# First h phase of a fused attention and gated feed-forward kernel rearranged: single PSUM banks, two early output accumulators, and the general loop from batch 2

## The chip, the cores and the metric

The kernel runs on one core of one Trainium2 chip. The metric is the device time of one execution in microseconds (us); the median of several runs is compared. "PE" is the matmul engine (TensorE) and "PEld" its weight load, "DVE" is VectorE, "ACT" is ScalarE, "POOL" is GpSimd, "SP" is SyncE, which only issues DMAs here. PSUM has eight banks; a bank holds 512 fp32 values for each of 128 partitions.

## The reference

There are 8 batches, 8 heads, 576 rows and 64 columns in a head. A small set p of 32 packed rows attends to k and v, and q then attends to the packed rows. The result, laid out as 4608 x 512, goes through a feed-forward of width 2048 with the gate h·cos(h).

```
def sm_attn(qq, kk, vv):
    s = scale * np.matmul(qq, kk.transpose(0, 1, 3, 2))
    a = exp(s - max(s));  a = a / sum(a)
    return np.matmul(a, vv)
p_packed = sm_attn(p, k, v)                  # 8 x 8 x 32 x 64
x = sm_attn(q, p_packed, p_packed)           # as 4608 x 512
h = x @ w_in                                 # 512 x 2048
out = (h * np.cos(h)) @ w_out                # 2048 x 512
```

## The kernel before

**Stages of one batch b.** The kernel never forms x. It makes, in this order:

- kT, qT: k and q with the head dimension on partitions. Two ways: `pe_T` (L94, 24 PE transposes in three groups of eight, each group copied from PSUM by the engine named) or `xbar` (L90, one DMA transpose issued by SP).
- `s1(b)` (L133): scores of p against k, then exp on ACT into a1, with row sums; `recips(b)` (L143): two small DVE instructions.
- a1T: a1 transposed, by PE (`a1_pe` L154, `a1_one` L164) or by a DMA transpose (`a1_xbar` L149).
- `permute_v(b)` (L85): one copy of v into another order, vp, on POOL (on DVE for batch 0).
- `pp(b)` (L172): 24 matmuls of 64 columns from vp and a1T, evacuated to ppT by four small copies.
- `ppw(b, n)` (L189): ppT times columns n*512 to n*512+512 of w_in, 8 matmuls, evacuated to PPW. Four of them for each batch.
- `s2(b)` (L215): scores of q against the packed rows, exp to a2u; `sums2` (L222): column sums by a matmul with ones, then Ln; `normalise(b)` (L232): two exps on ACT and two products on DVE give a2n.
- `h_mm(b, fc)` (L242), for fc = 0 to 15: four matmuls of 288 columns give h for 128 of the 2048 columns and 576 rows in a pair of PSUM banks; ACT makes cos (L254), DVE multiplies (L257) into gT. After fc 7 and fc 15 POOL copies the last 64 rows of two batches side by side into `joint` (L261).
- output chunks (`out_gen`, L295): a chunk is 128 rows, 16 matmuls of 512 columns over fc into one bank, then a copy to osb and the DMAs to the output from SP. A batch has four chunks; an odd one has a fifth, from `joint`, for two batches. One output matmul is one unit of filler: `fill(n)` issues n of them between the other work.

**Order.** The instructions of each engine run in program order; there is no scheduler. PSUM is shared by pool `psA` (three pairs of banks, L50), which serves nearly everything, and pool `psO` (two single banks, L51), for output chunks and, at the start, for `bank()` users (`own=True`).

**Opening** (L343 to L396): loads, batch 0 up to a2n, batch 1 up to a1T. `warm` issues dummy matmuls. All loads go through POOL's DMA queue in program order. The times at which POOL issues them show that it waits for the landing of the eighth load before (the issue of w_out's third quarter, at 19.91 us, is released by w_in's first quarter, for example).

**h phase of batch 0** (L397 to L408): 16 times `h_mm(0, fc)`, with ppw(0, 1..3) behind fc 1, 5, 8, pp(1) behind 10, the transposes of q of batch 1 behind 11 to 13, `set_filler(0)` behind 13, and two filler units behind 14 and 15.

**Front of batch 1** (L431 to L448): s2, ppw, sums2, normalise for batch 1, with 22 units of filler; k of batch 2, q of batch 2 and k of batch 3 go through `xbar`.

**Slot of batch 1** (L449, `slot` L410): 16 times h_mm(1, fc) with filler of batch 0 shared out between them and hooks behind given fc.

**Stage of batch 2** (L452 to L483): written by hand. It makes s1, a1T, pp, s2, ppw of batch 2 and also s1 and a1T of batch 3, with 80 units of filler of batch 1, and then runs the slot of batch 2.

**General loop, from batch 3** (L485 to L516): s2(s), ppw(s, 2), the DMA transpose of q(s+1), 8 units, s1(s+1), ppw(s, 3), the DMA transpose of a1(s+1), the DMA transpose of k(s+2), a one-element copy `gate` on POOL that waits for that k, 9 units around sums2, normalise(s), 13 units, the loads of later batches, and the slot with pp(s+1) behind fc 5 and ppw(s+1, 0..1) behind fc 10. `permute_v(s + 1)` stands at the head of the loop.

Of the kernel before, what the change touches and what calls it, by code (L numbers as in the profile page):

```python
# [15 lines left out]
def kernel(  # L16
# [38 lines left out]

    w_in_bf = const.tile([128, 4, DF], BF16, name="w_in_bf")
# [19 lines left out]
            eng.tensor_copy(out=out, in_=in_)  # L76
# [164 lines left out]

    def h_mm(b, fc):  # L242
        if fc == 0:
            gT[b] = g_pool.tile([128, NFC, S], BF16, name="gT", tag="gT")
# [11 lines left out]
        def rest():  # L256
            V.tensor_tensor(out=gT[b][:, fc, :].rearrange("p (e x) -> p e x", e=2),  # L257
                            in0=ps[:, :, 0:HS], in1=csv, op=ALU.mult)
# [182 lines left out]
    xbar("k", 2)  # L441
    xbar("q", 2)
    xbar("k", 3)
    G.tensor_copy(out=gate, in_=xT["k", 3][0:1, 0, 0:1])
    load("q", 3)
# [3 lines left out]
    slot(1, [(3, lambda: pw2(1, 2, (ACT, V))), (6, lambda: pack_p(2, 5)), (8, lambda: pack_p(5, B)),  # L449
             (8, lambda: (permute_v(2), load("v", 3), load("k", 4)))], 4)  # L450

    fill(1000)  # L452
    set_filler(1)
    ACT.preload_act_table_set(EXP_SET)
    s1(2)
    fill(10)
# [3 lines left out]
    recips(2)  # L460
    fill(3)
    s1(3)
    pp(2)
    a1_xbar(3)
    recips(3)
    fill(6)
    s2(2)
    ppw(2, 0, V)
    xbar("q", 3)
    xbar("k", 4)  # L470
    fill(4)
    sums2(2, 0)
    ppw(2, 1, V)
    sums2(2, 1)
    normalise(2)
    G.tensor_copy(out=gate, in_=a2n[2][0:1, 1, 0:1])
    permute_v(3)
    fill(8)
    G.tensor_copy(out=gate, in_=xT["k", 4][0:1, 0, 0:1])
    for n, b in (("v", 4), ("q", 4), ("k", 5)):  # L480
        load(n, b)
    fill(8)
    slot(2, [(3, lambda: pw2(2, 2, (ACT, V))), (7, lambda: pp(3, engs=(ACT, ACT))), (11, lambda: pw2(3))], 5, {11: 3})  # L483

    for s in range(3, B):  # L485
        nxt = s + 1 < B
        fill(1000)
# [8 lines left out]
        fill(8)
        if nxt:
            s1(s + 1)
            ppw(s, 3, V)
            a1_xbar(s + 1)  # L500
            recips(s + 1)
            if s + 2 < B:
                xbar("k", s + 2)
                G.tensor_copy(out=gate, in_=xT["k", s + 2][0:1, 0, 0:1])
# [45 lines left out]
```

## Time and profile before

| what | value |
|---|---|
| time, median of 3 runs | 254.6 us (254.18, 254.6, 256.1) |
| profiled execution: span from first to last instruction | 252.3 us (its only own time) |
| PE / ACT / DVE / POOL busy, share of the span | 92% / 68% / 65% / 23% |
| granted TensorE clock, mean over the span | 0.997 |
| loads by POOL's queue, each k, q or v (576 KB) | 8 each, median 12.2 / 9.6 / 7.4 us to landing |
| the four quarters of w_in, of w_out (512 KB) | 16.5, 20.9 us to landing (median) |
| DMA transposes of k, q, a1 | 6, 6, 5; median 5.3, 6.6, 4.0 us to landing |

Times of a position are us from the start of the span. A row of the timeline has the start, the length, the engine, the source line, the instruction with its operands, its count, and in brackets how long the engine had been idle before it and what released it. Several instructions in a row are merged; since matmuls are pipelined, the length of the last one overlaps what follows. A row of the table of windows gives, for a stretch of the span, its length and then the busy time and the count of instructions of each engine, the granted TensorE clock as a share, the busy share of the DMA engines, and GB/s.

### The profile page before, as it was taken

How to read it: one execution, taken by the hardware profiler on the slowest of the kernel's cores; microseconds unless marked ns; L12 is line 12 of the kernel's file. 1: busy time of each engine (PE TensorE's matmuls, PEld its weight loads, DVE VectorE, ACT ScalarE, POOL GpSimd, SP SyncE). 2: the span in 40 equal slices, each digit the busy share in tenths (PEclk: the TensorE clock that was granted, in tenths of full speed). 3: DMA queues.
4: the chain of work that ended last, by engine and by line, in shares of the span. 5: the costliest groups of instructions: out<-in, count | busy, mean ns of one | idle time of the engine just before them, and what ended most of it. 6: DMA issues, size and time to landing. Idle time of an engine off the chain costs nothing.

```text
span 252.3 us, 4989 instructions
## 1 busy us (share of the span) xinstructions
PE 233.3 (92%) x1981; PEld 130.7 (52%) x2014; DVE 163.0 (65%) x245; ACT 170.5 (68%) x285; POOL 58.4 (23%) x71
## 2 busy tenths in 40 slices
PE   8786888999969999999999998999899999999993
PEld 3453463566435554465446553565356554665452
DVE  2548996789376977477847675479556874876110
ACT  2366888857558788878886667887877585873000
POOL 8442604200362243104313105020500000000000
PEclk9999999999999999999999999999999999999998
DMA  6999999999999989999999994979471112112133
GB/s 91 202 211 205 205 207 226 200 186 149 191 208 198 176 175 212 220 204 164 225 173 181 180 182 99 175 141 196 97 144 44 42 44 70 36 34 62 50 83 83
DMA packets 65270, 37.67 MB, mean 149 GB/s; under 512 B 37872, under 2 KB 60656, under 8 KB 65248
## 3 DMA queue, kind: packets, MB, share of 16 engines
q0 software_dynamic: 23184, 18.81, 48.8%
q1 hardware_dynamic: 41904, 18.42, 36.8%
q8 instruction: 15, 0.25, 0.4%
q10 hardware_dynamic: 160, 0.13, 0.2%
q14 instruction: 7, 0.06, 0.1%
HBM read 37.22 MB, written 9.44 MB: 185 GB/s over the span
## 4 chain that ended last, share of the span: by engine, by line
PE 74%; DVE 8%; ACT 7%; DMA 5%; issue 2%; POOL 2%; DVEq 0%; POOLq 0%; ACTq 0%
PE ot L303 42%; PE psA L250 22%; DMA w_in_bf<-in_moe_w_in_dram 5%; DVE gT L257 5%; PE psA L201 3%; ACT cosT L254 3%; PE psA L177 2%; PE psA L227 1%; PE ot L289 1%; ACT a2u L219 1%; ACT L489 1%; DVE rs L147 1%; PE psA L128 1%; DVE osb L76 1%; DVE PPW L76 1%
## 5 line engine op out<-in xcount | busy, mean ns | idle before, releaser
L303 PE MATMUL ot<-w_out_bf,gT 128*128 128x512 bf16 x483 | 126.9, 380 | 2.1 <-issue 1.3
L257 DVE TENSOR_TENSOR gT<-psA,cosT 128x576 bf16<-128x576 f32 x128 | 94.1, 754 | 31.1 <-ACT cosT L254 30.0
L254 ACT ACTIVATE cosT<-psA 128x576 bf16<-128x576 f32 x128 | 82.7, 652 | 29.8 <-PE psA L250 28.1
L250 PE MATMUL psA<-a2n,PPW 128*128 128x288 bf16 x512 | 84.0, 286 | 2.5 <-DVE PPW L76 1.0
L303 PEld LDWEIGHTS <-gT 128*128 128x128 bf16 x512 | 48.0, 98 | 42.6 <-issue 6.1
L250 PEld LDWEIGHTS <-PPW 128*128 128x128 bf16 x512 | 49.1, 98 | 36.5 <-issue 3.8
L76 DVE CAST PPW<-psA 128x1024 bf16<-128x1024 f32 (+1 forms) x23 | 25.8, 1128 | 12.1 <-PE psA L201 12.1
L261 POOL COPY joint<-gT 128x512 bf16<-128x512 bf16 x16 | 9.8, 614 | 88.7 <-DVE gT L257 88.7
L76 DVE COPY osb<-ot 128x512 f32<-128x512 f32 (+1 forms) x19 | 12.8, 671 | 16.9 <-PE ot L303 13.8
L74 ACT COPY osb<-ot 128x512 f32<-128x512 f32 (+1 forms) x18 | 10.3, 571 | 18.7 <-PE ot L303 14.1
L76 POOL COPY vp<-vbf 96x3072 bf16<-96x3072 bf16 x7 | 19.2, 2750 | 1.6 <-DMA vbf<-in_v_dram 1.6
L237 DVE SCALAR_TENSOR_TENSOR a2n<-a2u,r,lns 128x576 bf16<-128x576 bf16 x16 | 12.4, 813 | 9.6 <-ACT lns L235 9.6
L229 ACT ACTIVATE lns<-psA 128x576 f32<-128x576 f32 x16 | 10.3, 651 | 5.7 <-PE psA L227 5.3
L137 ACT ACTIVATE a<-psA 128x576 bf16<-128x576 f32 x16 | 10.2, 648 | 5.0 <-PE psA L128 5.0
L303 PE MATMUL ot<-w_out_bf,joint 128*128 128x512 bf16 x46 | 12.4, 380 | 0.1
L201 PE MATMUL psA<-w_in_bf,ppT 64*32 64x512 bf16 x224 | 10.4, 381 | 1.5 <-DVE gT L257 1.1
L219 ACT ACTIVATE a2u<-psA,rs 128x576 bf16<-128x576 f32 x16 | 11.0, 736 | 1.2 <-PE psA L128 1.1
L254 ACT ACT_TABLE_LOAD x8 | 10.3, 1283 | 0.1
L74 ACT CAST ppT<-psA 64x128 bf16<-64x128 f32 x24 | 6.2, 259 | 6.1 <-PE psA L103 2.9
L235 ACT ACTIVATE lns<-lns 128x576 f32<-128x576 f32 x16 | 10.0, 678 | 0.0
L341 PE MATMUL ot<-wz 128*128 128x512 bf16 x24 | 8.1, 472 | 1.5 <-DVE wz L353 1.2
L74 ACT CAST PPW<-psA 128x1024 bf16<-128x1024 f32 (+1 forms) x9 | 7.2, 826 | 2.6 <-PE psA L201 2.6
(71 smaller groups left out, 143.4 us busy)
## 6 DMA issues: line engine op xcount, KB each, us to landing
kbf<-in_k_dram POOLq DMA_DIRECT2D x8, 576.0 KB, 12.2
vbf<-in_v_dram POOLq DMA_DIRECT2D x8, 576.0 KB, 7.4
qbf<-in_q_dram POOLq DMA_DIRECT2D x8, 576.0 KB, 9.6
out_dram<-osb SPq DMA_DIRECT2D x24, 192.0 KB, 2.6
out_dram<-osb SPq DMA_DIRECT2D x22, 128.0 KB, 2.4
w_in_bf<-in_moe_w_in_dram POOLq DMA_DIRECT2D x4, 512.0 KB, 16.5
w_out_bf<-in_moe_w_out_dram POOLq DMA_DIRECT2D x4, 512.0 KB, 20.9
out_dram<-osb SPq DMA_DIRECT2D x26, 64.0 KB, 2.1
```

What stands on the lines that cost most here:

```text
L74: ACT.copy(out=out, in_=in_)
L76: eng.tensor_copy(out=out, in_=in_)
L137: ACT.activation(out=a1[b % 2][:, y, :, 0:TP].rearrange("p (e m) x -> p e m x", e=2), in_=ps[y][:, :, 0:HS].rearrange("p e (m x) -> p e m ...
L201: nc.tensor.matmul(ps[y][32 * x:32 * x + 32, :], ppT[b % 2][r, 2 * x + y, :], w_in_bf[r, x, n * 512:(n + 1) * 512], start=True, stop=True)
L219: ACT.activation(out=a2u[b][:, y].rearrange("p (e x) -> p e x", e=2), in_=ps[y][:, :, 0:HS], func=AF.Exp, scale=rs1[b][:, y:y + 1])
L229: ACT.activation(out=lns[b][:, y].rearrange("p (e x) -> p e x", e=2), in_=ps[:, :, 0:HS], func=AF.Ln)
L235: ACT.activation(out=lns[b][:, y], in_=lns[b][:, y], func=AF.Exp, scale=-1.0)
L237: V.scalar_tensor_tensor(out=a2n[b][:, y], in0=a2u[b][:, y], scalar=r1[b][:, y:y + 1], in1=lns[b][:, y], op0=ALU.mult, op1=ALU.mult)
L250: nc.tensor.matmul(ps[:, e, 0:HS], PPW[b][:, y, fc * 128:(fc + 1) * 128], a2n[b][:, y, e * HS:(e + 1) * HS], start=(y == 0), stop=(y == 1))
L254: ACT.activation(out=csv, in_=ps[:, :, 0:HS], func=AF.Sin, bias=PI_HALF)
L257: V.tensor_tensor(out=gT[b][:, fc, :].rearrange("p (e x) -> p e x", e=2), in0=ps[:, :, 0:HS], in1=csv, op=ALU.mult)
L303: nc.tensor.matmul(pss[c], w, w_out_bf[:, fc, :], start=(fc == 0), stop=(fc == NFC - 1))
```

## The change

**PSUM.** `psA` can be closed and opened again. `banks(3)` gives three pairs as before; `banks(1)`, in force only during the h phase of batch 0, gives one pair and four single banks (`psH`).

**h phase of batch 0.** `h_one` takes the first 512 rows only: two matmuls of 512 columns into one single bank, cos and product on 512. The other 64 rows are made later by one `h_rest(0)`: 32 matmuls of 64 columns into one pair, one cos and one product of 1024, straight into `joint` (so batch 0 needs no POOL copies). pp(1) and the transposes of q of batch 1 leave the phase. `set_filler(0)` moves to behind fc 3, and one filler unit follows each of fc 4 to 11: the two output banks hold chunks 0 and 1 from there on. ppw(0, 2) and ppw(0, 3) use the psA pair.

**Loads.** The first quarter of w_out moves ahead of the third and fourth of w_in; v of batch 1 moves behind w_in; k of batch 2 and the rest of p move ahead of the other three quarters of w_out.

**Opening.** The transposes of q(0) and k(1) go to the two single banks; normalise(0) and s1(1) stand ahead of ppw(0, 0).

**Front of batch 1.** It now also makes pp(1), the PE transposes of q(1) and k(2), s1(2), recips(2), a1T(2) by PE. It has 11 units of filler. Only q(2) and k(3) go through `xbar`.

**Slot of batch 1.** Hooks: ppw(1, 2..3) behind fc 1, h_rest(0) behind 4, pack_p behind 6, pp(2) behind 9, ppw(2, 0..1) behind 12. It has the 45 units left of batch 0.

**General loop from batch 2.** The stage written by hand is gone. In the loop, permute_v(3) does not stand at the head for s = 2 but behind normalise(2); on POOL it thus follows the gate copy that waits for k of batch 4.

```diff
-    A = ctx.enter_context(tc.tile_pool(name="psA", bufs=3, space=PSUM))
+    def banks(pairs):
+        psum["stack"].close()
+        psum["A"] = psum["stack"].enter_context(tc.tile_pool(name="psA", bufs=pairs, space=PSUM))
+        if pairs < 3:
+            psum["H"] = psum["stack"].enter_context(tc.tile_pool(name="psH", bufs=6 - 2 * pairs, space=PSUM))
...
+    def h_one(b, fc):
+        if fc == 0:
+            g_tile(b)
+        ps = psum["H"].tile([128, 512], FP32, name="psH", tag="H")
+        for y in range(2):
+            nc.tensor.matmul(ps, PPW[b][:, y, fc * 128:(fc + 1) * 128], a2n[b][:, y, 0:512],
+                             start=(y == 0), stop=(y == 1))
+        cs = cos_pool.tile([128, 512], BF16, name="cosT")
+        ACT.activation(out=cs, in_=ps, func=AF.Sin, bias=PI_HALF)
+        V.tensor_tensor(out=gT[b][:, fc, 0:512], in0=ps, in1=cs, op=ALU.mult)
+
+    def h_rest(b):
+        t = psa()
+        for fc in range(NFC):
+            for y in range(2):
+                nc.tensor.matmul(t[:, fc // 8, (fc % 8) * 64:(fc % 8) * 64 + 64],
+                                 PPW[b][:, y, fc * 128:(fc + 1) * 128], a2n[b][:, y, 512:576],
+                                 start=(y == 0), stop=(y == 1))
+        cs = cos_pool.tile([128, 2, 512], BF16, name="cosR", bufs=1)
+        ACT.activation(out=cs, in_=t, func=AF.Sin, bias=PI_HALF)
+        j0 = (b % 2) * 64
+        V.tensor_tensor(out=joint[b // 2][:, :, j0:j0 + 64],
+                        in0=t.rearrange("p a (f x) -> p (a f) x", x=64),
+                        in1=cs.rearrange("p a (f x) -> p (a f) x", x=64), op=ALU.mult)
...
-    for n in range(3):
-        load_w_in(n)
+    load_w_in(0)
+    load_w_in(1)
+    load_w_out(0)
...
+    load_w_in(2)
+    load_w_in(3)
     load("v", 1)
-    load_w_in(3)
...
-    pe_T("q", 0, (V, ACT, V))
+    pe_T("q", 0, (V, ACT, V), own=True)
     load("q", 1)
-    for n in range(4):
-        load_w_out(n)
+    load("k", 2)
     G.dma_start(out=p_raw[:, 4:, :], in_=p_rows[:, 4:, :])
+    for n in range(1, 4):
+        load_w_out(n)
...
-    load("k", 2)
     permute_v(1)
+    banks(1)
     for fc in range(NFC):
-        h_mm(0, fc)()
-        if fc in (1, 5, 8):
-            ppw(0, 1 + fc // 4, (ACT, V), own=True)
-        if fc == 10:
-            pp(1, own=True, engs=(ACT, ACT))
-        if fc in (11, 12, 13):
-            pe_T("q", 1, (V, ACT, V), (fc - 11,), own=True)
-        if fc == 13:
+        h_one(0, fc)
+        if fc in (1, 5, 9):
+            ppw(0, 1 + fc // 4, (ACT, V), own=fc == 1)
+        if fc == 3:
             set_filler(0)
-        if fc >= 14:
-            fill(2)
+        if 4 <= fc < 12:
+            fill(1)
+    banks(3)
...
+    pp(1)
     ACT.preload_act_table_set(EXP_SET)
+    pe_T("q", 1, (V, ACT, V))
     s2(1)
+    load("v", 2)
     load("q", 2)
     load("k", 3)
-    load("v", 2)
     dup_p(4, 2 * B, G)
-    fill(8)
+    ppw(1, 0, V)
+    pe_T("k", 2, (V, ACT, V))
     sums2(1, 0)
     sums2(1, 1)
...
+    pack_p(2, 5)
+    fill(2)
+    normalise(1)
+    s1(2)
+    recips(2)
     ppw(1, 1, V)
-    normalise(1)
-    fill(14)
...
+    fill(6)
     a1_pe(2, (0,))
     fill(3)
     a1_pe(2, (1,))
...
+    xbar("q", 2)
+    xbar("k", 3)
+    def behind_k3():
+        permute_v(2)
+        load("v", 3)
+        G.tensor_copy(out=gate, in_=xT["k", 3][0:1, 0, 0:1])
+        load("q", 3)
+        load("k", 4)
+    behind_k3()
+    slot(1, [(1, lambda: pw2(1, 2, (ACT, V))), (4, lambda: h_rest(0)), (6, lambda: pack_p(5, B)),
+             (9, lambda: pp(2, engs=(ACT, ACT))), (12, lambda: pw2(2))], 4, {12: 2})
-    for s in range(3, B):
+    for s in range(2, B):
...
-        if nxt:
+        if nxt and s > 2:
             permute_v(s + 1)
...
         normalise(s)
+        if s == 2:
+            permute_v(3)
         fill(13)
```

More of the change, by code (lines that the diff above doesn't have):

```diff
@@ L49 @@
     small = ctx.enter_context(tc.tile_pool(name="small", bufs=3))
-    A = ctx.enter_context(tc.tile_pool(name="psA", bufs=3, space=PSUM))
     O = ctx.enter_context(tc.tile_pool(name="psO", bufs=2, space=PSUM))
     ctx.enter_context(tc.manual_schedule())
+    psum = {"stack": ctx.enter_context(ExitStack())}
+    def banks(pairs):
[4 more added lines that the diff above has]
+    banks(3)
     V, ACT, G = nc.vector, nc.scalar, nc.gpsimd
@@ L78, in psa @@
     def psa(dt=FP32):
-        return A.tile([128, 2, 512 if dt == FP32 else 1024], dt, name="psA", tag="A")
+        return psum["A"].tile([128, 2, 512 if dt == FP32 else 1024], dt, name="psA", tag="A")
     def load(n, b):
@@ L243, in h_mm @@
         if fc == 0:
-            gT[b] = g_pool.tile([128, NFC, S], BF16, name="gT", tag="gT")
-            if b % 2 == 0:
-                joint[b // 2] = j_pool.tile([128, NFC, 128], BF16, name="joint", tag="joint")
+            g_tile(b)
         ps = psa()
@@ L263, in h_mm, with g_tile @@
         return rest
+    def g_tile(b):
+        gT[b] = g_pool.tile([128, NFC, S], BF16, name="gT", tag="gT")
+        if b % 2 == 0:
+            joint[b // 2] = j_pool.tile([128, NFC, 128], BF16, name="joint", tag="joint")
+    def h_one(b, fc):
+        if fc == 0:
+            g_tile(b)
+        ps = psum["H"].tile([128, 512], FP32, name="psH", tag="H")
[18 more added lines that the diff above has]
+                        in1=cs.rearrange("p a (f x) -> p (a f) x", x=64), op=ALU.mult)
     n_out = [0]
@@ L374 @@
     pp(0)
-    pe_T("q", 0, (V, ACT, V))
+    pe_T("q", 0, (V, ACT, V), own=True)
     load("q", 1)
-    for n in range(4):
+    load("k", 2)
+    G.dma_start(out=p_raw[:, 4:, :], in_=p_rows[:, 4:, :])
+    for n in range(1, 4):
         load_w_out(n)
-    G.dma_start(out=p_raw[:, 4:, :], in_=p_rows[:, 4:, :])
     s2(0)
@@ L384 @@
     sums2(0, 1)
-    pe_T("k", 1, (V, V, V))
+    pe_T("k", 1, (V, V, V), own=True)
     pack_p(1, 2, bank(BF16))
     warm(2)
+    normalise(0)
+    s1(1)
     cut_ppw, rest_ppw = ppw(0, 0, V, own=True, later=True, cuts=((0, 128), (128, 512)))
-    normalise(0)
     cut_ppw()
-    s1(1)
     a1_one(1)
@@ L394 @@
     recips(1)
-    load("k", 2)
     permute_v(1)
+    banks(1)
     for fc in range(NFC):
-        h_mm(0, fc)()
-        if fc in (1, 5, 8):
-            ppw(0, 1 + fc // 4, (ACT, V), own=True)
-        if fc == 10:
-            pp(1, own=True, engs=(ACT, ACT))
-        if fc in (11, 12, 13):
-            pe_T("q", 1, (V, ACT, V), (fc - 11,), own=True)
-        if fc == 13:
+        h_one(0, fc)
+        if fc in (1, 5, 9):
+            ppw(0, 1 + fc // 4, (ACT, V), own=fc == 1)
+        if fc == 3:
             set_filler(0)
-        if fc >= 14:
-            fill(2)
+        if 4 <= fc < 12:
+            fill(1)
+    banks(3)
     def slot(s, hooks, keep=0, heavy={}):
@@ L429, in tk @@
         return lambda: pe_T(n, b, (V, V, V), (i,))
+    pp(1)
     ACT.preload_act_table_set(EXP_SET)
+    pe_T("q", 1, (V, ACT, V))
     s2(1)
-    ppw(1, 0, V)
+    load("v", 2)
     load("q", 2)
     load("k", 3)
-    load("v", 2)
     dup_p(4, 2 * B, G)
-    fill(8)
+    ppw(1, 0, V)
+    pe_T("k", 2, (V, ACT, V))
     sums2(1, 0)
     sums2(1, 1)
[L441 to L445, printed above, removed]
-    ppw(1, 1, V)
-    normalise(1)
-    fill(14)
[L449 to L456, printed above, removed]
+    pack_p(2, 5)
[3 more added lines that the diff above has]
+    recips(2)
+    ppw(1, 1, V)
+    fill(6)
     a1_pe(2, (0,))
@@ L459 @@
     a1_pe(2, (1,))
[L460 to L483, printed above, removed]
-    for s in range(3, B):
+    xbar("q", 2)
[10 more added lines that the diff above has]
+    for s in range(2, B):
         nxt = s + 1 < B
```

## The prediction

> **What bounds the kernel now.** I read the page's busy shares first, then the chain that ended last, then a table of windows cut at the stage borders, then the timelines of PE, SP, POOL and DVE around them.
>
> ```profile
> PE 233.3 (92%) x1981; PEld 130.7 (52%) x2014; DVE 163.0 (65%) x245; ACT 170.5 (68%) x285; POOL 58.4 (23%) x71
> ...
> PE 74%; DVE 8%; ACT 7%; DMA 5%; issue 2%; POOL 2%; DVEq 0%; POOLq 0%; ACTq 0%
> ```
>
> PE is 92% busy and 74% of the chain: time is lost only where PE stands still. The windows say where (busy times there are lengths of pipelined matmuls, so they hide short gaps).
>
> ```profile
> 22.70:40.10 17.40, 14.30 (x168) 8.48 (x167) 15.50 (x26) 14.40 (x26) 6.03 (x6) 1.00 1.27 206
> 40.10:45.70 5.60, 5.44 (x33) 2.51 (x35) 3.95 (x4) 4.88 (x8) 2.44 (x4) 1.00 1.25 221
> 45.70:63.90 18.20, 17.71 (x133) 10.77 (x133) 15.04 (x22) 11.89 (x20) 1.60 (x2) 1.00 1.32 179
> 63.90:79.40 15.50, 12.91 (x144) 6.25 (x147) 9.21 (x14) 10.38 (x20) 6.57 (x8) 1.00 1.09 200
> 79.40:98.40 19.00, 18.39 (x162) 10.80 (x164) 14.60 (x20) 14.98 (x26) 5.84 (x6) 1.00 1.13 185
> ...
> 123.90:152.30 28.40, 28.08 (x233) 15.53 (x236) 19.02 (x27) 20.30 (x35) 6.50 (x8) 1.00 1.02 176
> ```
>
> Rows: h phase 0; front 1; slot 1; front and slot of the hand-written stage 2; stage 4 of the general loop. PE is open in the first (DVE 15.5 of 17.4 us) and the fourth; stage 4 is nearly closed.
>
> ```profile
> 24.60 0.75 DVE L257 TENSOR_TENSOR gT<-psA,cosT 128x576 bf16<-128x576 f32 x1
> ...
> 38.86 0.76 DVE L257 TENSOR_TENSOR gT<-psA,cosT 128x576 bf16<-128x576 f32 x1 [0.17 <-ACT cosT L254]
> ```
>
> h phase 0 runs on DVE from 24.6 to 39.6: 0.94 us for each of 16 column blocks.
>
> ```profile
> 71.44 0.76 PEld L177 LDWEIGHTS <-vp 96*128 96x128 bf16 x24 [2.52 <-POOL vp L76]
> ```
>
> The largest single PE wait of stage 2: pp(2) waits for permute_v(2) on POOL. Now the general loop, stage 4, which begins with s2 at 123.86:
>
> ```profile
> 123.86 0.44 PE L128 MATMUL psA<-qT,ppT 64*32 64x288 bf16 x16
> ...
> 137.53 0.86 PE L177 MATMUL psA<-a1T,vp 96*128 96x64 bf16 x24
> ```
>
> ```profile
> 125.58 3.48 SPq L92 DMA_TRANSPOSE qT<-qbf  x1
> 129.15 1.98 SPq L151 DMA_TRANSPOSE a1T<-a  x1
> 131.24 3.05 SPq L92 DMA_TRANSPOSE kT<-kbf  x1
> ```
>
> ```profile
> 124.51 2.75 POOL L76 COPY vp<-vbf 96x3072 bf16<-96x3072 bf16 x1
> 136.30 0.18 POOL L504 COPY gate<-kT 1x1 bf16<-1x1 bf16 x1 [9.03 <-DMA kT<-kbf]
> ```
>
> pp comes 13.7 us after the stage's s2, the POOL gate 12.4 after it; the vp copy is long done, because it stands ahead of the gate.
>
> **The change, part by part.** Pitches on PE, from merged rows: filler 0.216 us (13 in 2.97, less a lone 0.38, over 12); h_mm 0.49, ppw 0.34, pp 0.70 (pieces of the chain); a matmul of 64 columns 0.029 (0.70 over 24); 24 transposes 1.03 (from 1.19); s1 or s2 0.26 to 0.35; a1T by PE 0.35 for each half; sums2 0.25; six pack transposes 0.34. DVE: 576-wide products follow each other every 0.67 us (two in 1.41, less 0.76), 512-wide PPW copies every 0.60 (29.73 to 30.33); a 512-wide product I take as 0.60. ACT: cos 0.55 pitch, at 512 wide about 0.49.
>
> *A, opening to 24.6: 0.* Load order: POOL's issues at 19.91, 22.41, 24.97 and 27.91 mark landings of w_in's first three quarters and v(1), 2.5 us for a quarter, 2.9 for a k, q or v. In the new order: w_in 1 and 2 at 19.8 and 22.3 as before, w_out's first quarter 24.9, w_in 3 and 4 at 27.5 and 30.0, v(1) 32.9 (before 27.9), q(1) 35.8, k(2) 38.7, rest of p 40.8, the w_out quarters 43.4, 46.0, 48.6, then v(2) 51.4, q(2) 54.3, k(3) 57.2. The new order of normalise(0), s1(1), ppw(0, 0), and k(1) through two single banks, shift things by 0.2 us at most either way.
>
> *B, h phase 0: −3.1 us.* DVE has 16 × 0.60 + 3 × 0.60 = 11.4 us in place of 16 × 0.67 + 3 × 0.60 + two q copies of 0.5. Four single banks: one tile's round is about 0.6 (two matmuls with their latency) + 0.6 cos + 0.7 product + 0.4 hand-overs = 2.3, over four 0.58: just under 0.60, so DVE sets the pace. I add 0.5 for ppw(0, 2), whose w_in lands at 27.5 when DVE is in column block 4. End 24.6 + 11.4 + 0.5 = 36.5 against 39.6. PE: 16 × 0.43 + 1.0 + eight units 1.7 lie inside. Ends: pitch 0.58 and no stall, −3.9; the old 0.94, 0.
>
> *C, front 1: +6.3 us.* Before it took 6.1 us from 39.6 to 45.7, with 22 units to cover its waits. Now 11 units, and a chain of ACT, DVE and PE with three PSUM pairs: pp(1) can start when vp(1) is ready (32.9 + 2.75 = 35.7) and its DVE copies after the last product, 36.8 to 37.5; ACT copies 37.5 to 38.1; table load 1.28 to 39.4; ACT copy of q 0.8 to 40.2; s2(1) and its exps (1.37) to 42.2; k(2) transposes take the pairs that these free, their ACT copy 42.7 to 43.5; Ln 43.5 to 44.7 with a wait; normalise 1.25 to 46.0; exps of s1(2) to 47.4; recips 47.7; the DVE copy of ppw(1, 1) behind them, 1.22, to 48.9, and its pair is what h_mm(1, 0) needs: slot 1 starts at 48.95. PE's own work there is pp 0.70, transposes 2.06, s1 and s2 0.65, ppw 0.68, sums 0.5, pack 0.34, units 2.4, a1T 0.70 = 8.0 of 12.45 us. Ends: PE-paced, 8.5 us (+2.4); 1.5 us more (+7.9).
>
> *D, slot 1: +3.6 us.* 16 × 0.49 + 45 × 0.216 + four ppw 1.36 + pack 0.34 + pp(2) 0.70 + h_rest 32 × 0.03 = 0.96: 20.9, against 17.4 before (38 units, two ppw, two packs), plus the 0.8 that slot 1 left open before, plus 0.1 for h_rest's pair held by a cos and a product of 1024 (like the 1.22 us PPW copy). T2, the first s2 of the general loop, is 48.95 + 21.8 = 70.75. Ends ±0.7.
>
> *E, stage 2: −6.1 + 3.0 us.* Before: 63.9 to 98.4, 34.5 us. As a stage of the general loop with five chunks it should take stage 4's 28.4, and the wait above goes. But on POOL permute_v(3) is now queued behind the gate for k(4), and pp(3), behind fc 5, needs it. SP must first do q(3), which waits for s2(2), then a1(3), then k(4). The gate came 12.4, 14.7 and 14.05 us after s2 in stages 4, 3 and 5 (136.30, 113.10, 166.35 less 123.86, 98.38, 152.30), mean 13.7; plus 0.2 and the 2.75 us copy plus a hand-over, vp(3) is ready 16.7 after s2, and pp stands at 13.7. PE waits 3.0, with all of the slot behind it, and nothing gives that back. Behind permute_v(3) on POOL the loads of v(4), q(4), k(5) go out some 17 us into the stage; q(4) is first wanted 30 us in, so they are covered (0). The DMA work ahead fits: xbar q(2) from 54.4 beside two loads (5.8 us like that of 55.85) to 60.3, k(3) to 63.5, gate 65.4, loads of q(3) and k(4) then, some 6 to 9 us to land, against T2 + 1.7 = 72.5 when SP wants q(3). Ends of the wait: 1.7 from the earliest gate; 8 if q(3) lands 5 us late (its longest load took 17.8).
>
> [...] The longest PE wait of that window is 2.2 us with the granted clock at 1.00. [...]
>
> *Sum:* −3.1 + 6.3 + 3.6 − 6.1 + 3.0 = +3.7 us. Cross-check: 70.75 + 28.4 + 3.0 = 102.15 against 98.4. From there on both programs are alike. Against the span of 252.3 this is 256.0; the page has no other time of its execution, and the runs' median is 254.6, 2.3 above the span. Predicted: 254.6 + 3.7 = 258.3 us.
>
> **Rivals.**
> - *Front 1 is paced by PE* (not slower). Place: 36.5 to 48.95. Price: part C falls by up to 3.9, total 254.4; with the POOL wait at its low end 253.1, and without it 251.4. It decides when slot 1 begins before 45.2. For it: transposes and units could fill. Against: only 11 units, and ACT alone has 8.7 us of work there in sequence.
> - *The single banks don't shorten h phase 0.* If latency, not DVE, set 0.94 us, B is 0: 261.4. Against: the round of 2.3 us over four banks.
> - *Loads late, and the POOL wait long.* q(3) or k(4) lands 5 us late, the wait is 8: 263.3. For it: DMA share 1.09 to 1.32 throughout. Against: the transpose of k(2), 7.04 us on SP from 48.64, is gone from that queue.
> - *No wait at pp(3)*: the gate fires by 10.8 us after s2: 255.3. Against: no gate did so early in three stages.
>
> **How the numbers follow.** Chances: the forecast, slower by about 3.7, 0.45; PE-paced front 0.22 (half of it below −1%); no wait 0.08; h phase unshortened 0.08; late loads 0.17. A measurement of this kernel tells about 1% from no change, 252.1 to 257.1. Faster 0.12 (half of the first rival and a little); same 0.27 (its rest, no wait, and the forecast's low edge); slower 0.61. The forecast's own range is 256 to 260.5. The range that leaves out 2 in 10 goes from the first rival with a short wait to the late loads: 252.5 to 263.
>
> **What would show it.** In the changed profile: last product of h phase 0 at 36.5 (B); first 288-column h matmul near 49 (C), with PE rows there released by ACT and DVE copies; second-stage s2 near 70.8 (D); the row of pp(3) with POOL vp as releaser, near 84.4, after an idle of some 3 us, and the gate 13.7 us after s2 (E). I am wrong if slot 1 begins at 46 or earlier, or if the pp(3) row has no wait.

## The result, and the profile after

The changed kernel takes 265.94 us (median of 4, 265.26 to 266.33) against 254.95 us of the kernel before beside it (4 runs, 254.18 to 256.1): a ratio of 1.0437, interval 1.0397 to 1.0476. It is 11.0 us slower; 3.7 us were forecast. The profiled execution took 266.33 us, with a span of 264.2 against 252.3 before.

First the page: busy shares, the chain that ended last, and the granted clock in 40 slices.

```profile
PE 238.9 (90%) x2004; PEld 132.8 (50%) x2038; DVE 164.6 (62%) x247; ACT 171.5 (65%) x286; POOL 57.3 (22%) x68
...
PEclk9999995799999979999999999999999999999999
...
PE 67%; DVE 10%; ACT 9%; DMA 8%; issue 2%; POOL 2%; SPq 0%; DVEq 0%; ACTq 0%; POOLq 0%
```

PE's share of the chain falls from 74% to 67%. The clock, 9 in all slices but the last before, now dips at slices 7 and 8 (some 40 to 53 us) and 15 (some 92 to 99 us). Now the windows, cut at the borders that answer to those of the prediction: opening, h phase 0, front 1, slot 1, stage 2. The clock is the third figure from the end.

```profile
22.70:26.71 4.01, 2.91 (x21) 1.08 (x21) 1.96 (x6) 1.91 (x3) 1.50 (x2) 1.00 1.24 206
26.71:38.30 11.59, 8.27 (x48) 3.04 (x49) 11.58 (x19) 9.72 (x18) 4.28 (x3) 1.00 1.29 215
38.30:54.56 16.26, 11.95 (x152) 7.86 (x153) 9.84 (x14) 9.77 (x16) 6.65 (x6) 0.69 1.27 204
54.56:76.79 22.23, 21.22 (x200) 12.73 (x203) 17.90 (x25) 14.75 (x25) 2.33 (x4) 1.00 1.22 136
76.79:110.40 33.61, 30.11 (x234) 16.41 (x238) 18.81 (x26) 22.41 (x37) 6.51 (x8) 0.95 0.88 164
```

| part | before | after | measured | forecast |
|---|---|---|---|---|
| A, first product of h phase 0 | at 24.60 | at 26.71 | +2.1 | 0 |
| B, h phase 0 | 15.0 | 11.6 | −3.4 | −3.1 |
| C, front 1, to the first h matmul of slot 1 | 6.1 | 16.3 | +10.2 | +6.3 |
| D, slot 1 | 18.2 | 22.2 | +4.0 | +3.6 |
| E, stage 2, to the s2 of stage 3 | 34.5 | 33.6 | −0.9 | −3.1 |
| sum at the s2 of stage 3 | 98.38 | 110.40 | +12.0 | +3.7 |

Behind that point the programs are alike: the spans differ by 11.9 us.

**Part A.** The ACT rows at the start of the h phase: in brackets, the idle time before and its releaser. First the kernel before, then the changed one, and then the changed kernel's first h matmul on PE.

```profile
21.81 1.28 ACT L254 ACT_TABLE_LOAD   x1
23.42 0.65 ACT L254 ACTIVATE cosT<-psA 128x576 bf16<-128x576 f32 x1 [0.33 <-PE psA L250]
```

```profile
24.79 1.28 ACT L285 ACT_TABLE_LOAD   x1 [2.40 <-PE psA L177]
26.08 1.09 ACT L285 ACTIVATE cosT<-psH 128x512 bf16<-128x512 f32 x2
```

```profile
24.13 1.32 PE L282 MATMUL psH<-a2n,PPW 128*128 128x512 bf16 x3 [0.65 <-DVE a1T L84]
```

No code places either sine table load; each has the line of the first cosine. Before, ACT began it at 21.81, right behind the last exp, with the cosine itself at 23.42, so it was hidden. Here the load is released by PE at 24.79, with ACT idle for 2.40 us ahead of it, so 1.28 us of loading stand on the path. In the trace an EVENT_SEMAPHORE instruction of the cosine's line, from 24.11 to 24.76, stands ahead of this load. The other sine loads of the two profiles have none and begin without a wait (at 50.72 in the changed kernel, for a cosine at 55.25).

The remaining 0.8 us has two parts. The chain ahead runs 0.6 us late (DVE's last copies of PPW come at 23.99, before at 23.41): PE waited 0.49 and 0.41 us for DVE's copies of k(1) out of two single banks, and s1(1) came at 20.62 (19.90). And the first h matmul waits 0.65 us for DVE's copy of a1T, which it does not read: the bank that the new pool gives it is one that a1T's transposes have just used. Before, it stood at 22.73, with no wait.

**Part B.** DVE's rows of the h phase, first and last group of products.

```profile
26.71 1.29 DVE L286 TENSOR_TENSOR gT<-psH,cosT 128x512 bf16<-128x512 f32 x2 [1.43 <-ACT cosT L285]
...
34.62 3.68 DVE L286 TENSOR_TENSOR gT<-psH,cosT 128x512 bf16<-128x512 f32 x6
```

No row in the phase has an idle time behind the first: DVE sets the pace, at about 0.60 us for a product, as forecast.

**Part C.** The PE rows at the two ends of front 1.

```profile
38.35 0.86 PE L185 MATMUL psA<-a1T,vp 96*128 96x64 bf16 x24 [1.81 <-DVE gT L286]
...
54.56 0.65 PE L256 MATMUL psA<-a2n,PPW 128*128 128x288 bf16 x4 [1.89 <-DVE PPW L84]
```

pp(1) was forecast to have its matmuls done by the end of the last product. Its vp was ready at 35.78, yet it begins behind that product: reopening three pairs puts pp(1)'s pair over banks that the last products still read. At the other end slot 1 waits for DVE's copy of PPW. DVE and POOL there:

```profile
50.73 0.17 DVE L154 RECIPROCAL r<-sums 128x2 f32<-128x2 f32 x1 [0.44 <-ACT a L145]
50.93 2.46 DVE L155 TENSOR_SCALAR rs<-r 128x2 f32<-128x2 f32 x1
53.30 1.21 DVE L84 CAST PPW<-psA 128x1024 bf16<-128x1024 f32 x1
```

```profile
50.62 2.75 POOL L84 COPY vp<-vbf 96x3072 bf16<-96x3072 bf16 x1 [5.84 <-DMA vbf<-in_v_dram]
```

A TENSOR_SCALAR of two columns takes 2.46 us, until POOL's copy of v(2) is over at 53.37. Its twin for batch 1, at 25.11, took 0.17. The kernel before has such a row too, beside POOL's copy of v(2) at 68.64 to 71.39:

```profile
68.90 2.52 DVE L147 TENSOR_SCALAR rs<-r 128x2 f32<-128x2 f32 x1
```

And the clock of the changed kernel, in windows of 3.41 us cut at its changes (the second figure is PE's busy time):

```profile
36.32:39.73 3.41, 1.60 (x42) 1.00 1.19 242
39.73:43.14 3.41, 1.82 (x36) 0.50 1.24 207
43.14:46.56 3.42, 2.99 (x40) 0.50 1.26 210
46.56:49.97 3.41, 3.05 (x36) 0.50 1.30 200
49.97:53.38 3.41, 2.70 (x21) 1.00 1.32 204
90.93:94.34 3.41, 0.74 (x16) 1.00 0.13 30
94.34:97.75 3.41, 3.41 (x26) 0.50 0.42 44
97.75:101.17 3.42, 3.37 (x23) 1.00 1.30 198
```

TensorE ran at half clock from 39.73 to 49.97, most of front 1, and from 94.34 to 97.75.

**Part E.** pp(3) on PE, and what it waits for on POOL.

```profile
93.96 1.19 PE L185 MATMUL psA<-a1T,vp 96*128 96x64 bf16 x24 [2.67 <-POOL vp L84]
```

```profile
91.05 0.18 POOL L524 COPY gate<-kT 1x1 bf16<-1x1 bf16 x1 [13.55 <-DMA kT<-kbf]
91.17 2.74 POOL L84 COPY vp<-vbf 96x3072 bf16<-96x3072 bf16 x1
```

This is the wait that was forecast: the gate fires 14.3 us after s2 (forecast 13.7), vp is ready 17.1 after it (16.7), and PE idles 2.67 us (3.0). What was left out is the half clock behind it.

### The profile page after: what moved, and what is told of

Read it like the earlier page. It is cut to its first block, busy times and chain, and to the rows that moved or that the text cites. A ratio compares the mean times of both kernels' runs of the same rounds, so it can differ in the third digit from the quotient of the medians.

```text
span 264.2 us, 5032 instructions
## 1 busy us (share of the span) xinstructions
PE 238.9 (90%) x2004; PEld 132.8 (50%) x2038; DVE 164.6 (62%) x247; ACT 171.5 (65%) x286; POOL 57.3 (22%) x68
## 3 DMA queue, kind: packets, MB, share of 16 engines
q1 hardware_dynamic: 39568, 17.83, 34.5%
## 4 chain that ended last, share of the span: by engine, by line
PE 67%; DVE 10%; ACT 9%; DMA 8%; issue 2%; POOL 2%; SPq 0%; DVEq 0%; ACTq 0%; POOLq 0%
PE ot L341 38%; PE psA L256 18%; DMA p_raw<-in_p_dram 5%; DVE gT L286 4%; DMA kT<-kbf 3%; PE psA L185 2%; PE psA L209 2%; DVE gT L263 2%; ACT a2u L227 2%; DVE PPW L84 2%; ACT L509 1%; PE psA L235 1%; PE ot L327 1%; PE psA L136 1%; POOL vp L84 1%
## 5 line engine op out<-in xcount | busy, mean ns | idle before, releaser
L341 PE MATMUL ot<-w_out_bf,gT 128*128 128x512 bf16 x483 | 129.6, 382 | 2.0 <-issue 1.0
L263 DVE TENSOR_TENSOR gT<-psA,cosT 128x576 bf16<-128x576 f32 x112 | 83.1, 756 | 35.9 <-ACT cosT L260 35.1
L260 ACT ACTIVATE cosT<-psA 128x576 bf16<-128x576 f32 x112 | 72.8, 652 | 31.0 <-PE psA L256 29.0
L256 PE MATMUL psA<-a2n,PPW 128*128 128x288 bf16 x448 | 73.8, 287 | 2.4 <-DVE PPW L84 2.1
L256 PEld LDWEIGHTS <-PPW 128*128 128x128 bf16 x448 | 44.0, 98 | 33.3 <-issue 4.1
L84 DVE CAST PPW<-psA 128x1024 bf16<-128x1024 f32 (+1 forms) x24 | 27.1, 1132 | 13.4 <-PE psA L209 13.4
L245 DVE SCALAR_TENSOR_TENSOR a2n<-a2u,r,lns 128x576 bf16<-128x576 bf16 x16 | 12.4, 814 | 10.3 <-ACT lns L243 10.2
L341 PE MATMUL ot<-w_out_bf,joint 128*128 128x512 bf16 x47 | 12.6, 379 | 0.0
L209 PE MATMUL psA<-w_in_bf,ppT 64*32 64x512 bf16 x240 | 11.7, 398 | 0.8 <-ACT a2u L227 0.6
L185 PE MATMUL psA<-a1T,vp 96*128 96x64 bf16 x192 | 7.2, 196 | 4.7 <-POOL vp L84 2.7
L282 PE MATMUL psH<-a2n,PPW 128*128 128x512 bf16 x30 | 8.9, 381 | 2.3 <-ACT PPW L82 0.9
L286 DVE TENSOR_TENSOR gT<-psH,cosT 128x512 bf16<-128x512 f32 x16 | 10.0, 684 | 1.4 <-ACT cosT L285 1.4
## 6 DMA issues: line engine op xcount, KB each, us to landing
kbf<-in_k_dram POOLq DMA_DIRECT2D x8, 576.0 KB, 11.9
```

Of the source, the lines that this page charges most:

```text
L185: nc.tensor.matmul(ps[:, hp * 64:(hp + 1) * 64], vp[b][:, c, hp * 128:(hp + 1) * 128], a1T[b][0:TP, :, j, 32 * hp:32 * hp + 32], start=(j ...
L209: nc.tensor.matmul(ps[y][32 * x:32 * x + 32, :], ppT[b % 2][r, 2 * x + y, :], w_in_bf[r, x, n * 512:(n + 1) * 512], start=True, stop=True)
L245: V.scalar_tensor_tensor(out=a2n[b][:, y], in0=a2u[b][:, y], scalar=r1[b][:, y:y + 1], in1=lns[b][:, y], op0=ALU.mult, op1=ALU.mult)
L256: nc.tensor.matmul(ps[:, e, 0:HS], PPW[b][:, y, fc * 128:(fc + 1) * 128], a2n[b][:, y, e * HS:(e + 1) * HS], start=(y == 0), stop=(y == 1))
L260: ACT.activation(out=csv, in_=ps[:, :, 0:HS], func=AF.Sin, bias=PI_HALF)
L286: V.tensor_tensor(out=gT[b][:, fc, 0:512], in0=ps, in1=cs, op=ALU.mult)
```

## The experiments

Ratios are against the kernel before, run beside each. Positions are from the profiled execution.

**1. permute_v(3) at the head of stage 2** (in the changed kernel).

```diff
-        if nxt and s > 2:
+        if nxt:
             permute_v(s + 1)
...
-        if s == 2:
-            permute_v(3)
```

> The changed kernel with permute_v(3) back at the head of the loop, ahead of the POOL gate. Theory (the order on POOL costs the wait at pp(3), and the wait drops the granted clock): the 2.67 us wait goes and so does the stretch of half clock behind it (94 to 97.7), 1.2 to 1.6 us more; about 262 us against 265.9. Rival (the wait is really for a1T's transpose behind q(3) on SP): pp(3) still waits and the time stays within 1 us of 265.9. Second rival (the half clock has another cause): only 2.7 us are gained, 263.2.

Measured: 262.23 us, ratio 1.0306 (1.0249 to 1.0364). pp(3) at 91.19 has no wait, and the clock stays up there:

```profile
90.00:100.00 10.00, 9.95 (x94) 1.00 0.95 151
```

s2(3) comes at 105.97, 4.4 us earlier: 2.67 us of wait and some 1.7 us of half clock. Stage 2 without them takes 29.1 us, where 28.4 were forecast.

**2. v(2)'s POOL copy held until recips(2)** (in the changed kernel).

```diff
     def behind_k3():
+        G.tensor_copy(out=gate, in_=rs1[2][0:1, 0:1])
         permute_v(2)
```

> The changed kernel with permute_v(2) on POOL held, by the one-element gate copy, until recips(2) is done. Theory (the 2.46 us TENSOR_SCALAR of recips(2) is DVE standing still for POOL's copy, and slot 1 waits for it): that row falls to 0.17 us, slot 1 begins at 52.3 in place of 54.56, 263.6 us. Rival (something else ends as late, such as the a1T copies or the loads behind the held copy): under 1 us gained.

Measured: 264.46 us, ratio 1.0385 (1.0318 to 1.0452). DVE in front 1:

```profile
51.12 0.17 DVE L155 TENSOR_SCALAR rs<-r 128x2 f32<-128x2 f32 x1
51.20 1.22 DVE L84 CAST PPW<-psA 128x1024 bf16<-128x1024 f32 x1
```

The 2.3 us are gone, so the collision is their cause. Slot 1 begins only 1.4 us earlier (53.15), since PE's own queue, partly at half clock, lasts until 53.1.

**3. The sine table loaded ahead of the h phase** (in the changed kernel).

```diff
+    ACT.preload_act_table_set("trig_and_small")
     banks(1)
```

> The changed kernel with the sine table loaded on ACT right behind the exps of s1(1), as it was in the kernel before, and not with the first cosine's waits. Theory (the load, 1.28 us, stands on the path into h phase 0): its first product starts at about 25.4 in place of 26.71 and everything behind it moves by 1.3 us: 264.6. Rival (DVE or the loads set the end of the phase): the start moves and the last product stays at 38.3; no gain.

Measured: 265.01 us, ratio 1.0414 (1.0298 to 1.0529). The h phase ends 1.0 us earlier, recips(2) now comes before POOL's copy (0.17 us), and slot 1 and T2, the first s2 of stage 2, come 3.4 us earlier (51.18, 73.41). Of this only 0.8 is left at s2(3), 109.59. Where it goes, on PE and on POOL:

```profile
91.94 1.46 PE L185 MATMUL psA<-a1T,vp 96*128 96x64 bf16 x24 [4.04 <-POOL vp L84]
```

```profile
89.03 0.18 POOL L525 COPY gate<-kT 1x1 bf16<-1x1 bf16 x1 [14.91 <-DMA kT<-kbf]
```

PE arrives earlier, but the transpose of k(4), the gate and the copy come only 2.0 us earlier: the wait grows from 2.67 to 4.04 us. Behind it the clock is at half from 91.08 to 97.90, 6.8 us in place of 3.4, and from pp(3) to s2(3) another 1.2 us go.

**4. Eight filler units moved from the h phase into front 1** (in the changed kernel), four behind pp(1), four behind the transposes of q(1).

```diff
-        if 4 <= fc < 12:
-            fill(1)
...
     pp(1)
+    fill(4)
     ACT.preload_act_table_set(EXP_SET)
     pe_T("q", 1, (V, ACT, V))
+    fill(4)
```

> The changed kernel with the eight filler units of h phase 0 moved into front 1, four behind pp(1) and four behind the transposes of q(1). Theory (front 1 runs at half clock because PE has too little to do from 36.4 on, and its transposes and small matmuls on the chain take twice as long): the clock stays at 1.00 until 44 at least, front 1 shortens by some 1.5 us, 264.4 us. Rival (ACT and DVE pace front 1 at any clock): the clock recovers and the time stays within 0.5 us. If the clock still falls, the gap from 36.4 to 38.35 is enough by itself.

Measured: 266.22 us, ratio 1.0448 (1.0373 to 1.0522), not distinguishable from the changed kernel. The clock is at half from 38.48 to 41.89 only, and then at 1.00 to the end of front 1:

```profile
43.00:46.00 3.00, 2.16 (x50) 1.47 (x49) 1.83 (x3) 1.85 (x3) 2.79 (x4) 1.00 1.24 207
```

Yet slot 1 begins at 54.47, as in the changed kernel: TENSOR_SCALAR comes 12.7 us behind the last product (12.6 in the changed kernel), again stands beside POOL's copy (2.66 us) and ends with it. So the half clock is not by itself what paces front 1; v(2)'s landing and the copy behind it fix its end.

**5. pp(1) ahead of the bank switch, on top of experiment 1.**

```diff
+    pp(1)
     banks(3)
...
-    pp(1)
     ACT.preload_act_table_set(EXP_SET)
```

> The changed kernel with permute_v(3) at the loop's head (as in e1_head, 262.2 us) and pp(1) issued before the PSUM pools are switched back, so that it takes the one pair that is free and not a bank behind the last product. Theory (opening the three pairs makes pp(1) wait for the last product, 1.81 us of PE standing still, and puts its 0.86 us on the chain): pp(1) runs at about 36 when vp(1) is there, the chain of front 1 shortens by 0.9 us, recips(2) comes before POOL's copy at 50.6 and so loses its 2.3 us of standstill, and the half clock starts later or not at all: about 258.5 us. Rival (pp(1) is ready anyway, the chain is ACT's): under 0.5 us gained against e1_head.

Measured: 259.87 us, ratio 1.0199 (1.0121 to 1.0278). pp(1) runs at 36.64, recips(2) gets ahead of POOL's copy (its TENSOR_SCALAR comes 11.4 us behind the last product and takes 0.17 us, though the clock is at half from 40.86 to 47.69), slot 1 begins at 51.30, and s2(3) comes at 102.63. Against experiment 1 the gain of 3.3 us at the front is kept in full: with vp(3) early there is no wait to give it to.

**6. All of these edits together**, and the transposes of q(0) and k(1) in pairs again (filler as in the changed kernel).

```diff
-    pe_T("q", 0, (V, ACT, V), own=True)
+    pe_T("q", 0, (V, ACT, V))
...
-    pe_T("k", 1, (V, V, V), own=True)
+    pe_T("k", 1, (V, V, V))
```

> The changed kernel with all of it: permute_v(3) at the head, permute_v(2) held until recips(2) is done, the sine table early, pp(1) before the pools are switched back, and the transposes of q(0) and k(1) in pairs of psA as before. If the losses add: e1_head less 1.3 (sine) less 3.2 (pp(1) and recips) less 0.6 (transposes): 257 us. If they overlap, because front 1 ends with recips(2) and each of them only moves it past the POOL copy: 258.5 us. Either way not below the kernel before, since front 1 keeps its chain of some 11 us on ACT and DVE.

Measured: 257.04 us, ratio 1.0104 (1.0054 to 1.0153): from 1.0437, so some three quarters of the loss is recovered, not all. Its profiled execution took 261.07 us and the other three 256.66 to 257.39, so its trace does not explain their time. In that trace the first product of h phase 0 is at 24.82 (24.60 in the kernel before), and pp(3) again waits 2.99 us, now for the DMA transpose of a1(3).

**7. The kernel before, with permute_v(2) early on POOL**, to see what its own 2.2 us wait at pp(2) is worth.

```diff
+    permute_v(2)
     G.tensor_copy(out=gate, in_=xT["k", 3][0:1, 0, 0:1])
...
-             (8, lambda: (permute_v(2), load("v", 3), load("k", 4)))], 4)
+             (8, lambda: (load("v", 3), load("k", 4)))], 4)
```

> The kernel before with one move: permute_v(2) on POOL ahead of the gate that waits for k(3), in place of behind it. The same theory from the other side (a POOL copy queued behind a gate is what pp waits for): the 2.2 us wait of pp(2) goes, and with it the 2.52 us recips(2) that stood still beside that copy: 252.3 us against 254.3. Rival (s1(3) and the transpose of a1(3) pace the stage): under 0.5 us.

Measured: 257.48 us, ratio 1.0143 (1.0083 to 1.0202): slower, where 2 us less were expected. pp(2) moves from 71.44 to 69.23 without a wait and s2(3) from 98.38 to 96.31, as expected. Then PE and SP in stage 3:

```profile
112.84 1.44 PE L177 MATMUL psA<-a1T,vp 96*128 96x64 bf16 x24 [3.42 <-DMA a1T<-a]
```

```profile
104.87 3.77 SPq L92 DMA_TRANSPOSE qT<-qbf  x1
108.73 1.47 SPq L151 DMA_TRANSPOSE a1T<-a  x1
```

The loads of v(4), q(4) and k(5) still go out at 91.6 to 93.1, behind POOL's gate at 90.65 (90.34 before). That of q(4) takes 12.4 us to land (9.4 before), and its transpose begins 3.3 us later than before (at 101.57); why the load takes longer was not tested. So PE is 2.07 us earlier and the transposes are later. It waits 3.42 us, the clock's mean from 96.31 to 126.30 is 0.94, and the next s2 is at 126.58 (123.86 before): more than twice the gain is paid back. Whether the loads of v(4), q(4) and k(5) without the gate ahead of them would keep the gain, or a1(3) turned on TensorE would help experiment 6, stays open: neither was measured.

**8. Only the h phase of the change, in the kernel before**, with h_rest(0) behind fc 4 of slot 1 and the sine table loaded early.

```diff
+    ACT.preload_act_table_set("trig_and_small")
+    banks(1)
     for fc in range(NFC):
-        h_mm(0, fc)()
+        h_one(0, fc)
...
+    banks(3)
...
-    slot(1, [(3, lambda: pw2(1, 2, (ACT, V))), (6, lambda: pack_p(2, 5)), (8, lambda: pack_p(5, B)),
+    slot(1, [(3, lambda: pw2(1, 2, (ACT, V))), (4, lambda: h_rest(0)), (6, lambda: pack_p(2, 5)), (8, lambda: pack_p(5, B)),
```

> The kernel before with only the h phase of the change: single banks, 512-wide tiles, h_rest(0) in slot 1 behind fc 4, the sine table loaded early; opening, loads, hooks of the phase, front 1, stage 2 as before. By the prediction's part B: DVE has 16 x 0.60 + 3 x 0.60 + 2 x 0.5 = 12.4 us from about 25.3, the last product ends near 38 against 39.6, less 0.96 us of h_rest in slot 1: 0.6 us gained, 253.7. Rival (latency of the single banks, or the later start, takes it back): no gain or a loss up to 1 us.

Measured: 253.76 us against 254.06 (10 and 13 runs), ratio 0.9983 (0.9956 to 1.0011). The phase starts 1.0 us later (25.61), with the opening as before: the first h matmul again waits 0.65 us for the copy of a1T, and the clock is at half from 24.01 to 27.42. It ends at 39.62, as before, where 38 was expected; the hooks of pp(1) and of q(1) keep their place in it, and DVE waits for ACT's cosines there (0.24, 0.64 and 0.17 us). s1(2), behind slot 1, comes 2.0 us later, 1.7 of them in slot 1, which has h_rest. They are taken up by the slack at pp(2), which now stands at 71.23 with no wait.

**9. TensorE's clock and the VectorE collision by themselves.** The kernel leaves out the attention and writes zeros. Between stretches of `dense(60)`, full matmuls of 128x512, stand known pauses and thin loads; then rows of VectorE operations alone and beside POOL copies of v's form.

```diff
+    for n in (0, 1, 2, 3, 4, 6):
+        dense(60)
+        pause(n)
+    dense(60)
+    load(40)
...
+    for _ in range(4):
+        G.tensor_copy(out=vp.rearrange("p c (h d) -> p c h d", h=H),
+                      in_=big.rearrange("p (h c d) -> p c h d", h=H, c=6))
+    for _ in range(4):
+        row()
```

> No attention is computed: zeros are written, and the disputed costs are measured by themselves. Part 1: six times 60 matmuls of 512 columns, behind each a pause of TensorE of a known length (VectorE copies some 0, 1, 2, 3, 4 and 6 PSUM banks: pauses of about 0.5, 1.1, 1.7, 2.3, 2.9 and 4.1 us); then 40 small matmuls with a copy between each two (TensorE at a fifth), 60 matmuls, a pause of two copies, the 40 small ones again, 60 matmuls. Theory from the changed kernel's trace (a gap of 1.8 us was enough, and a thin load holds the clock down): the granted clock falls to half behind the pauses from 1.7 us on, each time for about 3.5 us of full matmuls, and behind the pause that the small matmuls follow it stays at half until the full matmuls have run about 3.5 us. Rival one (it takes a gap near 3 us, and the thin load is what lowered the clock in the changed kernel): only the pauses of 2.9 and 4.1 us lower it, and the 40 small matmuls lower it by themselves, with no pause ahead. Rival two: both are needed. Part 2: six kinds of VectorE operation, twice alone and then four times beside copies on POOL of v's shape and form (2.75 us each). Theory: the TENSOR_SCALAR of 128x2 takes 2.3 to 2.7 us where it falls beside a copy and 0.17 us alone, and the others that have all operands in SBUF stand likewise, while those that read PSUM pass; rival: any operation stands, so the 1.2 us copy from PSUM takes up to 4 us.

The pauses on PE were 0.28, 0.88, 1.60, 2.33, 3.05 and 4.49 us; only the last two lowered the clock, and so did the thin load without a pause. Windows around the pause of 2.33 us (59.38 to 61.71), the pause of 3.05 us (74.83 to 77.88), and the start of the thin load at 112.44:

```profile
57.47:60.88 3.41, 1.91 (x9) 1.00 0.00 0
60.88:64.30 3.42, 2.54 (x11) 1.00 0.00 0
74.54:77.95 3.41, 0.36 (x3) 1.00 0.00 0
77.95:81.37 3.42, 3.42 (x9) 0.50 0.00 0
112.09:115.50 3.41, 1.64 (x9) 1.00 0.00 0
115.50:118.91 3.41, 1.31 (x5) 0.50 0.00 0
```

My theory (1.7 us is enough) falls; the first rival, that a gap near 3 us is needed and that a thin load lowers the clock by itself, fits. The VectorE rows beside POOL's four copies (182.28 to 193.89):

```profile
182.52 2.70 DVE L92 TENSOR_SCALAR rs<-r 128x2 f32<-128x2 f32 x1
185.26 0.17 DVE L93 RECIPROCAL r<-rs 128x2 f32<-128x2 f32 x1
185.34 2.81 DVE L94 COPY z<-y 128x512 bf16<-128x512 bf16 x1
188.07 0.41 DVE L95 TENSOR_TENSOR z<-x,y 128x512 bf16<-128x512 bf16 x1
188.52 0.69 DVE L96 TENSOR_TENSOR x<-pq,y 128x512 bf16<-128x512 f32 x1
189.24 1.22 DVE L97 CAST x<-pq 128x1024 bf16<-128x1024 f32 x1
```

Alone the six take 0.16, 0.17, 0.27, 0.42, 0.69 and 1.22 us. So TENSOR_SCALAR and COPY within SBUF stand until the running POOL copy ends, and the two that read PSUM (0.69 and 1.22) pass. RECIPROCAL passes too: in the changed kernel it took 0.17 us at 50.73, inside POOL's copy. For the product of two SBUF operands the row shows less: it starts at 188.07 together with the third POOL copy, and that copy took 3.02 us where the second and the fourth took 2.74. It may be the copy that stood. Whether such a product stands inside a running copy was not measured.

**10. Pauses of 2.4 to 3.2 us, and front 1's own forms of matmul, by themselves** (again without the attention).

```diff
+    dense(60)
+    rest(3, 1)
...
+    turn(192)
+    dense(60)
+    probs(192)
+    dense(60)
+    parts(160, 288)
...
+    duty(24, 1)
+    dense(60)
+    duty(16, 2)
```

> No attention is computed: zeros are written, and the kinds of TensorE work of front 1 are measured by themselves. Between stretches of 60 full matmuls (128x512) stand: three pauses, of about 2.45, 2.65 and 2.9 us; then without any pause 192 back-to-back transposes of 96x96, 192 matmuls of 64 columns (the probabilities' form), 160 of 64 rows by 32 with 288 columns (the scores' form), 80 of the same with 512 columns (PPW's form); then 24 single full matmuls with a VectorE copy between each two, and 16 pairs with a copy behind each. Theory (the clock falls where TensorE does little array work over some 3 us, and small operands count as little): the pauses of 2.65 and 2.9 us lower it and 2.45 does not; the transposes and the 64-column matmuls lower it to half about 3 us after they start though TensorE never waits, and with them the front's own work held the clock down in the changed kernel; the two forms of 64 by 32 and the pairs keep it at 1.00. Rival (only idle time counts): the clock stays at 1.00 in all four forms without a pause, and falls at the single matmuls, if at all.

The pauses came out as 2.39, 2.78 and 3.15 us, and all three lowered the clock. The 192 transposes, the 64-column matmuls and both forms of 64 by 32 kept it at 1.00; single matmuls with copies between lowered it, pairs did not. Here the theory's half on small operands falls, and with it that a pause of some 2.45 us would be harmless. Windows of the pause of 2.39 us, of the single matmuls, and of the pairs:

```profile
17.01:20.42 3.41, 1.02 (x6) 0.99 0.00 0
20.42:23.83 3.41, 3.41 (x10) 0.51 0.00 0
23.83:27.25 3.42, 3.42 (x17) 1.00 0.02 5
...
143.34:146.75 3.41, 1.95 (x5) 0.98 0.02 5
146.75:150.17 3.42, 2.05 (x4) 0.50 0.00 0
...
180.88:184.30 3.42, 2.19 (x7) 1.00 0.00 0
```

The clock changes at fixed steps here: in the changed kernel 39.73, 49.97, 94.34 and 97.75 lie 3, 13 and 1 times 3.41 us apart, and in experiment 9 115.50 lies 11 such steps behind 77.95. In these profiles the next step's clock goes with how busy the profile has TensorE in the step just past. A pause of 2.39 us within one step leaves 1.02 of 3.41 us busy, 30%, and the next step is at half; one of 2.33 us astride two leaves 56% and 74% and costs nothing. The other rows shown are in line: at full clock, steps of 0.36, 0.74, 1.60 and 1.64 us (11, 22, 47 and 48%) were followed by half clock, and one of 2.19 us (the pairs, 64%) was not.

The border lies near 53% in these profiles. Steps of 1.78 us (from 20.38 in experiment 5) and 1.79 us (from 36.46 in experiment 3) were followed by half clock, and one of 1.81 us (from 43.85 in experiment 9) was not. Of the some 800 steps at full clock in the twelve profiles, two lie on the wrong side of it. One is the first step of single matmuls, 1.88 us from 143.23 (the row shown is cut 0.1 us later), which was followed by half clock; a lone matmul's row is 0.39 us long, where in the full stretches one follows another every 0.213 us. The other stands at the end of experiment 6 (1.58 us from 253.47, the clock kept).

To come back took more. At half clock the changed kernel's step of 2.99 us (88%) did not bring the clock back, the next, of 3.05 us (89%), did, and every full step did.

## Why the prediction was wrong

The direction and the place of the forecast wait were right. Three terms failed, A, C and E, each by something that the sum did not have at all. Measured less forecast is A +2.1, B −0.3, C +3.9, D +0.4, E +2.2, together +8.3, which is 12.0 less 3.7.

- **A, "0", was +2.1.** The step that fails is "shift things by 0.2 us at most either way". I followed the loads and the new order, and neither ACT's instruction before the first cosine nor the bank of the first h matmul. The table load that begins only when PE releases it costs its 1.28 us: in experiment 3, which places it by hand, the first product comes 1.31 us behind the first h matmul and not 2.58. The other 0.8, the late chain and the wait for the copy of a1T, was read in the trace and not tested by itself.
- **B, −3.1, was −3.4.** Right, and for the reason given: DVE, not the latency over four banks, sets the pace, so that rival falls. The 0.5 us added for ppw(0, 2) did not come. But experiment 8 shows that this part alone, in the kernel before, is worth nothing measurable.
- **C, +6.3, was +10.2.** That a chain of ACT, DVE and PE ends front 1 was right: PE waits for DVE at 54.56, and the rival of a front paced by PE falls. Two steps failed. One is "pp(1) can start when vp(1) is ready": vp(1) was ready at 35.78 as forecast, and pp(1) began at 38.35, behind the last product. TENSOR_SCALAR then came 12.6 us behind that product, against 11.4 with pp(1) early (experiment 5) and a forecast of 11.2 for recips(2). The other is the sum's last link, recips(2) and then the copy of ppw(1, 1): it has no standstill beside POOL's copy, though the kernel before has one (68.90). v(2) was forecast to land at 51.4, well behind recips(2) at 47.7. It landed at 50.6, TENSOR_SCALAR came at 50.9 and stood 2.3 us. Early pp(1) gave 3.3 us, these 2.3 included. Experiment 2 takes just the standstill away and gets 1.4 of it, as the half-clocked queue of PE is next. What the half clock adds to the chain was not separated.
- **D, +3.6, was +4.0.** Right.
- **E, "−6.1 + 3.0", was −0.9.** The wait itself was right (2.67 for 3.0, gate at 14.3 for 13.7), and experiment 1 confirms its cause. The term that the sum lacks is the half clock behind the wait, about 1.7 us (half of the step of 3.41 us at 94.34). Another 0.7 is the stage itself, 29.1 for 28.4. The prediction shows a wait of 2.2 us with the clock at 1.00 and counts nothing for the clock behind one of 3.0. In the changed kernel 2.67 us was enough to lower it, since 90.93 to 94.34 held only 0.74 us of work; the wait of 2.2 us in the kernel before left the clock at 1.00, with 1.95 us of work (57%) in its step, 70.04 to 73.45.
- **The sum itself.** Parts add up only while nothing absorbs them. Experiment 3 gained 3.4 us at T2 and kept 0.8; experiment 7 gained 2.07 in stage 2 and was 2.7 behind a stage later. Stage 2 is held by the chain of loads, SP's transposes, the gate and POOL's copy, which moves less than PE (2.0 of 3.4 us in experiment 3).

The price of the TENSOR_SCALAR's standstill is up to 2.5 us more for a small instruction: 2.70 us beside a POOL copy against 0.16 alone in experiment 9, and 2.46 beside the copy of 2.75 us in the changed kernel. Why it stands and RECIPROCAL does not, no run here shows.

Front 1 falls to half at 39.73, below the same border: its 1.81 us wait for the last product leaves 1.60 us, 47%, in the step before. The small operands need not come into it, as 64-column matmuls and transposes without a pause kept the clock at 1.00 in experiment 10.

**What stays open.** Why the single matmuls fall at 55%, so what in a matmul's row counts toward the border. Why the sine load of part A has a wait ahead of it. The last 1% of experiment 6: its 2.99 us wait for a1(3) is the largest of PE behind the opening, but the one trace is of an execution 4 us longer than the others.

## What to carry to other kernels

Forecast a wait with the load of TensorE around it, and add half a clock step (1.7 us here) where the gap leaves a 3.41 us step less than about half busy (0.74 us busy in the changed kernel's step from 90.93), and more where the next step is not full (6.8 us at half clock in experiment 3). Before counting a gain, follow the next stage's transfers and the copies that wait on them: if they do not move too, PE only waits longer, and the clock may make that a loss (experiment 7: 2.07 us gained, 2.7 behind a stage later). And look at which engine runs a copy beside the small instruction at the end of a chain: here a two-column operation of 0.17 us took 2.46 beside a copy of 2.75.
